# An RWKV-7 recurrence with a SoLU block: all chunk products in 64x64 tiles, transposes as products with the identity, banks taken in pairs

## The chip, the cores and the metric

One Trainium2 chip, and of it one core. The metric is the device time of one execution in microseconds (us). A core has a matrix engine (PE, which loads a stationary operand and streams a moving one, and writes to the PSUM banks), a vector engine (DVE), a scalar engine (ACT), a third elementwise engine (POOL), and queues that start DMA transfers (SP and ACT here). Each engine runs its instructions in the order in which they stand in its queue; semaphores tie the queues together.

## The reference

Inputs `r, k, v, w, a, b` have the shape (4 batches, 8 heads, 768 steps, 40). The first part is a recurrence over the steps, the second a block over 3072 tokens of width 320:

```python
for t in range(S):                       # state: (B, H, D, D)
    y[:, :, t] = einsum('bhd,bhde->bhe', rt, state)
    Sa = einsum('bhde,bhe->bhd', state, at)
    state = state * wt[:, :, None, :] - einsum('bhd,bhe->bhde', Sa, bt) + einsum('bhd,bhe->bhde', vt, kt)
x = y.transpose(0, 2, 1, 3).reshape(B * S, H * D)
h = x @ w_in                             # (320, 1024)
sm = softmax(h); solu = h * sm
ln = (solu - mean(solu)) / sqrt(var(solu) + 1e-6) * g_ln
out = ln @ w_out                         # (1024, 320)
```

The weights come as float64, and the kernel turns them into float32 itself.

## The kernel before, in words

Steps are cut into chunks of 64 (`C`). A **unit of work** is a pair of batches and one chunk: 128 partitions (two batches `p`, 64 steps each) by 8 heads. There are 2 x 12 = 24 such units (`N`), numbered i; i and i + 2 belong to the same pair of batches, so the state of i - 2 feeds i. Within a unit, 16 small products per step go over (p, head); a head is 4g + 2q + h in the kernel before.

The recurrence inside a chunk is solved in closed form. Per unit these helpers write the products, and PE runs them exactly in the order of the program (`manual_schedule`); the queues of DVE, ACT, POOL and SP are ordered by a scheduler when the program is built.

- `load_keys`, `load_values`: DMAs of w, b, k, a and of v, r, all from SP. `in_value_order`: three POOL copies that put v and r into the kernel's order of heads.
- `decay`: log of w (ACT), its running sum by a product with a triangle (bank `pcum`), its exponential (`inv`), the transposed running sum (`pex`) and its exponential (`ex`); POOL scales b and k (`kb`, line 285) and `front` sends that to DRAM (`kb_dram`).
- `front`: transposes b and a (`pbT`, `paT`, helper `turned`, line 291); ACT evicts `bT`, DVE evicts `aT` with a product (line 307).
- `norm`: products of b and a, masked by DVE (`nt`), written to DRAM and read back as `blk` in another layout (`spread`).
- `invert`: for every four units (`GRP`) DVE inverts 128 triangular 32x32 blocks by 30 rounds of `prod` (line 360) and `uu` (line 362); `bring` reads the results back as `tu` and `uh`, and `couple` (bank `py`) and `close` (bank `pz`) join the halves.
- `fetch`, `attend`: `kb` comes back as `kbx`; k, v, r are transposed (`pkT`, `pvT`, `prT`) and evicted by ACT. `scores`: their products (`ps`), masked by DVE into `psi` and the left part of `lv`. `states`: transposes the state (`psT`, line 518), evicted as `s`.
- `carried`, `driven` (bank `px`), `solved` (`pu`), `answered` (`pl`), `read` (`pyo`), `leave`: the solve, the output and the new state. `fence` is a drain of PE.
- `hidden` (`h`), `weighed`, `spreadof`, `folded` (`plnT`), `output` (`po`): the SoLU block of a unit that is done. It uses the whole 128x128 array, as the transposes do; the small products use the array as four 64x64 tiles.

A loop turn, called a **slot** here, does the stages of several units at once: `carried` to `leave` for unit i, `attend`, `couple`, `scores`, `close` for i + 1, `norm` for j = i + 7, `front` for j + 1, `decay` for j + 2, `hidden` for i - 1, `folded` and `output` for i - 2. PE's order in a slot before: px, pnt, px, plnT, pkT, pvT, prT, po, pu, py, h, pl, ps, pbT, paT, pcum, pex, psT, pyo, pz, pyo. A slot in which DVE has an inversion to do is called an inversion slot; inversions are started in slots 0, 4, 8, 12 and 16 (and one in the fill), and most of each runs in the slot after.

PSUM holds 8 banks of 512 floats per partition: `h` takes two, the other six go round among all the names above (`bank`, pool `ps1`). A product into a bank waits until the bank's last user has been read.

Of the kernel before, what the change touches and what calls it, by code (L numbers as in the profile page):

```python
# [45 lines left out]
def kernel(  # L46
# [34 lines left out]
    ps1 = ctx.enter_context(tc.tile_pool(name="ps1", bufs=6, space=PSUM))  # L81
# [32 lines left out]
    r_t = zeroed(nc.gpsimd, "r", [P, H, C], 2, pad)  # L114
    v_t = zeroed(nc.gpsimd, "v", [P, H, C], 2, pad)
# [12 lines left out]
    def bank(name):  # L128
        return ps1.tile([P, 512], FP32, tag="bank", name=name)
# [43 lines left out]
    def weights():  # L173
# [5 lines left out]
        pg = bank("pg")  # L179
# [6 lines left out]
        t = bank("pmean")  # L186
# [13 lines left out]
    units = [(p, g, q, h) for g in range(2) for p in range(2) for q in range(2) for h in range(2)]  # L200
# [16 lines left out]
    def pair(t, j):  # L217
        return t[:, j:j + 2, :].rearrange("p a b -> p (a b)")[:, 0:W2]
# [10 lines left out]
    def load(x, ap, i):  # L229
        bp, ci = where_(i)  # L230
        for p in range(2):
            nc.sync.dma_start(out=x[half(p), :, 0:D],
                              in_=ap[2 * bp + p, :, ci * C:(ci + 1) * C, :].rearrange("h t d -> t h d"))
# [5 lines left out]
    def load_keys(i):  # L239
        if not ok(i):  # L240
            return
        d = st[i]
        for n, ap in (("w", w), ("b", b), ("k", k), ("a", a)):
            x = a_t[i % 3] if n == "a" else two.tile([P, H, D], FP32, tag="raw_" + n, name="raw_" + n)
            d["raw_" + n] = x
            load(x, ap, i)

    def load_values(i):
        if not ok(i):
            return  # L250
        d = st[i]
        for n, ap in (("v", v), ("r", r)):
            d["raw_" + n] = two.tile([P, H, D], FP32, tag="raw_" + n, name="raw_" + n)
            load(d["raw_" + n], ap, i)

    def in_value_order(i):
        if not ok(i):
            return
        d = st[i]
        d["v"], d["r"] = v_t[i % 2], r_t[i % 2]  # L260
        d["lv"] = two.tile([P, H, W2], FP32, tag="lv", name="lv")
        for x, n in ((d["v"][:, :, 0:D], "raw_v"), (d["r"][:, :, 0:D], "raw_r"), (d["lv"][:, :, C:], "raw_v")):
            nc.gpsimd.tensor_copy(out=x.rearrange("p (h x) d -> p h x d", h=2),  # L263
                                  in_=d[n].rearrange("p (x h) d -> p h x d", h=2))


    def decay(i):
# [5 lines left out]
        t = bank("pcum")  # L273
        nc.tensor.matmul(heads(t[:, 0:DM]), lhsT=c_("cum"), rhs=lw[:, :, 0:D], start=True, stop=True)  # L274
        inv = two.tile([P, DM], FP32, tag="inv", name="inv", bufs=1)
        nc.scalar.activation(out=inv, in_=t[:, 0:DM], func=AF.Exp, scale=-1.0)  # L276
        t = bank("pex")
        for j in range(4):
            nc.tensor.matmul(t[0:W2, j * P:(j + 1) * P], lhsT=pair(lw, 2 * j), rhs=c_("cum"), start=True, stop=True)  # L279
        ex = d["ex"] = ex_t[i % (AHEAD + 3)]  # L280
        nc.scalar.activation(out=ex[0:W2, :, :, 1:].rearrange("p b j t -> p j b t"),
                             in_=t[0:W2].rearrange("p (j b t) -> p j b t", j=4, b=2), func=AF.Exp)
# [5 lines left out]
    def turned(name, src_, bufs=1, evict=True):  # L288
        t = bank("p" + name)
        for j in range(4):  # L290
            nc.tensor.transpose(out=t[0:W2, j * P:(j + 1) * P], in_=pair(src_, 2 * j), identity=ident)  # L291
        if not evict:
            return t
        o = two.tile([P, 4, P], FP32, tag=name, name=name, bufs=bufs)
        nc.scalar.copy(out=o[0:W2].rearrange("p j t -> p (j t)"), in_=t[0:W2])
        return o

    def front(i):
        if not ok(i):
            return  # L300
        d = st[i]
        nc.sync.dma_start(out=d["kb_dram"], in_=d["kbw"])
        ex = d["ex"]
        d["bT"] = turned("bT", d["kbw"][:, H:, :])
        t = turned("aT", d["raw_a"], evict=False)
        aT = d["aT"] = two.tile([P, 4, P], FP32, tag="aT", name="aT", bufs=AHEAD + 2)
        nc.vector.tensor_tensor(out=aT[0:W2].rearrange("p j (b t) -> p j b t", b=2),
                                in0=t[0:W2].rearrange("p (j b t) -> p j b t", j=4, b=2),
                                in1=ex[0:W2, :, :, 0:C].rearrange("p b j t -> p j b t"), op=ALU.mult)

    def masked(dst, t):
        nc.vector.tensor_tensor(out=dst, in0=t, in1=tri.unsqueeze(1).to_broadcast([P, 4, C]), op=ALU.mult)  # L312

    def keyed(t, i, u):
        p, g, q, h = u
        return t[rows(h), 2 * g + q, p * C:p * C + C]

    def valued(t, i, u):
        p, g, q, h = u
        return t[rows(q), 2 * h + g, p * C:p * C + C]  # L320

    def norm(i):
# [3 lines left out]
        t = [bank("pnt") for _ in range(2)]  # L326
        for u in in_turn(lambda p, g, q, h: (h, p ^ h)):
            p, g, q, h = u
            j = 2 * g + q
            mm(t[h][half(p ^ h), j * C:j * C + C], keyed(d["bT"], i, u), keyed(d["aT"], i, u))  # L330
        nt = d["nt"] = two.tile([P, 2, 4, C], FP32, tag="nt", name="nt", bufs=AHEAD + 1)
        for h in range(2):
            masked(nt[:, h], t[h][:, 0:256].rearrange("p (j c) -> p j c", j=4))
        d["nt_dram"] = dram.tile([P, H, C], FP32, tag="nt_dram", name="nt_dram", bufs=3)
# [35 lines left out]
    def bring(i):  # L370
# [6 lines left out]
        for x in range(2):  # L377
# [4 lines left out]
            nc.sync.dma_start(out=d["uh"][hi],  # L382
                              in_=uu[at + 16 + 8 * x:at + 24 + 8 * x, :, Q:].rearrange("h s t -> s h t"))

    def fetch(i):
# [3 lines left out]
        d["kb"] = two.tile([P, 2 * H, C], FP32, tag="kbx", name="kbx")  # L389
        nc.sync.dma_start(out=d["kb"], in_=d["kb_dram"])  # L390

    def couple(i):
# [3 lines left out]
        t = [bank("py") for _ in range(2)]  # L396
        for u in in_turn(lambda p, g, q, h: p ^ h):
            p, g, q, h = u
            j, x = 2 * g + q, half(p ^ h)
            mm(t[h][x, j * Q:j * Q + Q], d["nt"][x, h, j], d["tu"][x, 4 * h + j, 0:Q])  # L400
        for h in range(2):
            nc.scalar.activation(out=wy[:, h, :, 0:Q], in_=t[h][:, 0:4 * Q].rearrange("p (j c) -> p j c", j=4),
                                 func=AF.Copy, scale=c_("neg_hi"))

    def close(i):
# [3 lines left out]
        t = [bank("pz") for _ in range(2)]  # L409
        for u in in_turn(lambda p, g, q, h: p ^ h):  # L410
            p, g, q, h = u
            j, x = 2 * g + q, half(p ^ h)
            mm(t[h][x, j * Q:j * Q + Q], wy[x, h, j], d["uh"][x, 4 * h + j])
        for h in range(2):
            nc.scalar.copy(out=d["tu"][:, 4 * h:4 * h + 4, 2 * Q:], in_=t[h][:, 0:4 * Q].rearrange("p (j c) -> p j c", j=4))


    def attend(i):
# [3 lines left out]
        d["kT"] = turned("kT", d["kb"][:, 0:H, :])  # L422
        d["vT"] = turned("vT", d["v"])
        d["rT"] = turned("rT", d["r"], bufs=2)

    def scores(i):
# [3 lines left out]
        t = [bank("ps") for _ in range(2)]  # L430
        for u in in_turn(lambda p, g, q, h: (h, p)):
            p, g, q, h = u
            j = 2 * g + q
            mm(t[h][half(p), j * C:j * C + C], keyed(d["kT"], i, u), keyed(d["aT"], i, u))
        for u in in_turn(lambda p, g, q, h: (q, p)):
            p, g, q, h = u
            j = 4 + 2 * h + g
            mm(t[q][half(p), j * C:j * C + C], valued(d["vT"], i, u), valued(d["rT"], i, u))
        psi = d["psi"] = two.tile([P, 2, 4, C], FP32, tag="psi", name="psi")
        for x in range(2):  # L440
            masked(psi[:, x], t[x][:, 0:256].rearrange("p (j c) -> p j c", j=4))
        for x in range(2):
            masked(d["lv"][:, x::2, 0:C], t[x][:, 256:].rearrange("p (j c) -> p j c", j=4))


    def carried(i):
# [5 lines left out]
        d["px"] = [bank("px") for _ in range(2)]  # L452
        d["opened"] = set()
        if ci:
            for u in in_turn(lambda p, g, q, h: (h, p ^ h)):
                p, g, q, h = u
                j = 2 * g + q
                mm(d["px"][h][half(p ^ h), j * D:j * D + D], keyed(d["aT"], i, u),
                   st_t[bp][rows(h), 4 * p + j, 0:D], start=(h, p ^ h) not in d["opened"], stop=False)
                d["opened"].add((h, p ^ h))  # L460
            fence()

    def driven(i):
# [3 lines left out]
        for u in in_turn(lambda p, g, q, h: (p, p ^ h)):  # L467
            p, g, q, h = u
            j = 2 * g + q
            mm(d["px"][h][half(p ^ h), j * D:j * D + D], d["psi"][half(p), h, j],  # L470
               d["lv"][half(p), 4 * h + 2 * g + q, C:], start=(h, p ^ h) not in d["opened"])
            d["opened"].add((h, p ^ h))
        for h in range(2):
# [261 lines left out]
```

## Time and profile before

| | us |
|---|---|
| median of the runs | 824.64 (811.89 to 824.88, three runs) |
| the profiled execution | 821.3 |
| its span, first to last instruction | 819.5 |
| PE busy | 644.9 (79% of the span) |
| DVE, ACT, POOL busy | 379.0, 239.8, 168.4 |
| mean granted PE clock | 0.863 of full |

Every slot has one group of `pl` products, so their starts mark the slots. In the profile `pl` of unit 0 starts at 159.49, of unit 1 at 186.97, of unit 16 at 598.50, of unit 23 at 784.40. That cuts the span in four: a fill with one whole slot (187.0), 15 slots with everything in them (411.5, 27.4 each), 7 slots in which `norm`, `front` and `decay` have run out (185.9, 26.6 each), and a tail of 35.1.

A line of the timeline reads: start, length, engine, line, operation, output<-inputs, shape, how many were merged into the line, and in brackets how long the engine stood idle before and what released it. Matmuls overlap, so the step from one line's start to the next is what a group costs PE, not its length. A float32 product is two PE instructions; a PE transpose is one.

### The profile page before, as it was taken

The page shows a single profiled execution, that of the slowest core. Times are in us where ns is not written, and L with a number is a line of the kernel's source. Part 1 is how long each engine was busy: PE and PEld are TensorE (multiplying, and loading weights), DVE is VectorE, ACT ScalarE, POOL GpSimd, SP SyncE. Part 2 cuts the span into 40 slices and gives each one's busy share as a digit, 9 for nine tenths or more (in the row PEclk, how much of TensorE's full clock was granted, in tenths as well). Part 3 has the DMA queues.
Part 4 walks back from the last instruction along what each step waited for, and adds up shares of the span by engine and source line. Part 5 has one row for each costly group of instructions (what it writes and reads, how often), then busy time and mean ns, then how long its engine had stood idle before and what let it go on. Part 6 is the DMA issues. An engine that isn't in the chain of part 4 may idle for free.

```text
span 819.5 us, 26810 instructions
## 1 busy us (share of the span) xinstructions
PE 644.9 (79%) x11545; PEld 480.8 (59%) x11545; DVE 379.0 (46%) x1048; ACT 239.8 (29%) x592; POOL 168.4 (21%) x237
## 2 busy tenths in 40 slices
PE   4505506778989989889889899798997877989894
PEld 3304404657757766667667667676765665666652
DVE  3563572478403692343954228822479133123322
ACT  3323102323324322433234334133321222223121
POOL 6664234313202211221022102301111110000000
PEclk8655756669989989999989999799997789899997
DMA  7546847364464545554625655265422412011000
GB/s 149 145 133 138 204 109 191 64 138 95 96 169 108 111 79 129 155 122 89 146 80 115 152 133 127 49 161 125 97 70 52 120 47 54 23 52 41 15 20 13
DMA packets 224901, 84.31 MB, mean 103 GB/s; under 512 B 206088, under 2 KB 213136, under 8 KB 224016
## 3 DMA queue, kind: packets, MB, share of 16 engines
q1 hardware_dynamic: 220272, 76.12, 40.4%
q10 hardware_dynamic: 4512, 6.48, 2.7%
q8 instruction: 91, 1.49, 0.7%
q14 instruction: 26, 0.21, 0.1%
HBM read 49.53 MB, written 29.10 MB: 96 GB/s over the span
## 4 chain that ended last, share of the span: by engine, by line
PE 46%; DVE 23%; DMA 15%; issue 5%; POOL 5%; ACT 3%; SPq 2%; ACTq 0%; DVEq 0%; POOLq 0%
PE h L592 14%; PE po L642 10%; DMA kbx<-kb_dram 7%; DVE prod L360 5%; DVE uu L362 5%; PE pz L211 3%; PE pyo L211 3%; DVE e L604 3%; DVE nmax L595 3%; PE py L211 3%; DVE bs L612 2%; DMA uu_dram<-uu 2%; PE pu L211 2%; POOL n_s L143 2%; ACT e L598 2%
## 5 line engine op out<-in xcount | busy, mean ns | idle before, releaser
L595 DVE TENSOR_REDUCE nmax<-h 128x1 f32<-128x1024 f32 x24 | 29.4, 1223 | 305.0 <-PE h L592 305.0
L592 PE MATMUL h<-w_in,xT 120*128 120x512 f32 (+1 forms) x288 | 135.8, 622 | 0.0
L642 PE MATMUL po<-w,lnT 128*128 128x320 f32 x384 | 115.4, 456 | 3.9 <-ACT lnT L633 3.9
L642 PEld LDWEIGHTS po<-w,lnT 128*128 128x128 f32 x384 | 75.7, 203 | 34.9 <-ACT lnT L633 5.4
L592 PEld LDWEIGHTS h<-w_in,xT 120*128 120x128 f32 (+1 forms) x288 | 55.0, 197 | 62.2 <-issue 61.1
L598 ACT ACTIVATE e<-h,nmax 128x1024 f32<-128x1024 f32 x24 | 26.8, 1116 | 147.5 <-DVE nmax L595 147.5
L360 DVE TENSOR_TENSOR prod<-blk,uu 128x30 f32<-128x30 f32 (+9 forms) x180 | 62.9, 350 | 6.0
L362 DVE TENSOR_TENSOR uu<-uu,prod 128x30 f32<-128x30 f32 (+9 forms) x180 | 61.5, 342 | 5.7
L291 PE MATMUL pkT<-cst,kbx 128*104 128x128 f32 x96 | 18.7, 330 | 45.5 <-DMA kbx<-kb_dram 42.7
L621 POOL TENSOR_TENSOR rs<-c,mhalf 128x1 f32<-128x1 f32 x24 | 13.4, 557 | 188.7 <-DVE c L620 135.6
L285 POOL TENSOR_TENSOR kb<-raw_b,inv 128x320 f32<-128x320 f32 x24 | 20.9, 869 | 151.4 <-ACT inv L276 131.1
L291 PE MATMUL pbT<-cst,kb 128*104 128x128 f32 x96 | 18.4, 323 | 39.5 <-POOL kb L285 39.5
L263 POOL COPY v<-raw_v 128x320 f32<-128x320 f32 x24 | 10.9, 456 | 179.8 <-DMA raw_v<-in_v_dram 179.7
L274 PE MATMUL pcum<-lw,cst 128*128 128x320 f32 x48 | 24.6, 605 | 24.6 <-ACT lw L272 14.7
L211 PE MATMUL pyo<-lv,kbx 64*64 64x104 f32 x768 | 42.2, 268 | 0.5 <-DVE lv L312 0.4
L211 PE MATMUL pyo<-lu,kbx 64*64 64x104 f32 x768 | 41.0, 261 | 0.8 <-DVE lu L312 0.5
L291 PEld LDWEIGHTS pkT<-cst,kbx 128*104 128x104 f32 x96 | 12.2, 154 | 50.0 <-issue 46.9
L644 ACT ACTIVATE osb<-po,rs 128x320 f32<-128x320 f32 x24 | 12.7, 527 | 94.5 <-PE po L642 94.5
L211 PE MATMUL py<-tu,nt 64*64 64x32 f32 x768 | 30.6, 227 | 8.2 <-DMA tu<-uu_dram 6.0
L279 PEld LDWEIGHTS pex<-cst,lw 128*104 128x104 f32 x192 | 32.8, 223 | 7.0 <-issue 4.1
L474 ACT COPY x<-px 128x160 f32<-128x160 f32 x48 | 11.7, 295 | 83.7 <-PE plnT L632 25.4
L291 PEld LDWEIGHTS pbT<-cst,kb 128*104 128x104 f32 x96 | 11.4, 149 | 41.8 <-POOL kb L285 40.5
(105 smaller groups left out, 1253.1 us busy)
## 6 DMA issues: line engine op xcount, KB each, us to landing
kb_dram<-kb SPq DMA_DIRECT2D x24, 512.0 KB
kbx<-kb_dram SPq DMA_DIRECT2D x24, 512.0 KB
nt_dram<-nt SPq DMA_DIRECT2D x24, 256.0 KB
uu_dram<-uu SPq DMA_DIRECT2D x6, 1024.0 KB
raw_w<-in_w_dram SPq DMA_DIRECT2D x48, 80.0 KB
raw_b<-in_b_dram SPq DMA_DIRECT2D x48, 80.0 KB
raw_k<-in_k_dram SPq DMA_DIRECT2D x48, 80.0 KB
a<-in_a_dram SPq DMA_DIRECT2D x48, 80.0 KB
```

Of the source, the lines that this page charges most:

```text
L211: nc.tensor.matmul(o, lhsT=lhsT, rhs=rhs, start=start, stop=stop, skip_group_check=True)
L274: nc.tensor.matmul(heads(t[:, 0:DM]), lhsT=c_("cum"), rhs=lw[:, :, 0:D], start=True, stop=True)
L279: nc.tensor.matmul(t[0:W2, j * P:(j + 1) * P], lhsT=pair(lw, 2 * j), rhs=c_("cum"), start=True, stop=True)
L285: nc.gpsimd.tensor_tensor(out=kb[:, j * H:j * H + H, 0:D], in0=d["raw_" + n], in1=heads(inv), op=ALU.mult)
L291: nc.tensor.transpose(out=t[0:W2, j * P:(j + 1) * P], in_=pair(src_, 2 * j), identity=ident)
L360: nc.vector.tensor_tensor(out=t, in0=nb[:, j:j + 1, j + 1:Q].to_broadcast([P, j, m]), in1=u[:, 0:j, j:j + 1].to_broadcast([P, j, m]), op=A ...
L362: nc.vector.tensor_tensor(out=u[:, 0:j, j + 1:Q], in0=u[:, 0:j, j + 1:Q], in1=t, op=ALU.subtract)
L592: nc.tensor.matmul(h[:, hh], lhsT=d["xT"][0:n, kt, :], rhs=w_in[0:n, kt, hh], start=kt == 0, stop=kt == NK - 1)
L595: nc.vector.tensor_reduce(out=nmax, in_=h, axis=AX.X, op=ALU.max, negate=True)
L598: nc.scalar.activation(out=e, in_=h, func=AF.Exp, bias=nmax, accum_out=d["esum"])
L604: nc.vector.tensor_tensor(out=d["e"], in0=d["h"], in1=d["e"], op=ALU.mult)
L642: nc.tensor.matmul(o[:, 0:DM], lhsT=d["lnT"][:, f, :], rhs=w2[:, f, :], start=f == 0, stop=f == NF - 1)
```

## The change

- **Tiles.** The whole-array steps of the chunk work become 16 products of 64x64: each transpose is a product of the 64x64 block with a 64x64 identity (`turn`, `turned`), `pcum` becomes two products and `pex` 16. The state's transpose moves from `states` into `attend`. Only `plnT`, `h` and `po` still use the whole array, one after the other.
- **Banks.** `banks` hands out pairs of banks, three pairs in place of six single ones. Two tensors share a pair: k and v (`pkv`), r and the state (`prs`), a and b (`pa`), both halves of `plnT`. One instruction evicts both banks where there were two (masks, `nuT`, `lu`, `wy`, `tu`, `x`, `tot`).
- **Tiles of py and pz** alternate over four 64x64 tiles, not two.
- **Heads** are numbered 4q + 2g + h, so that v and r are loaded in place: `in_value_order` and its POOL copies go.
- **Buffers and transfers.** `kbx` gets a third buffer; `nt` is read back from DRAM (`ntx`) and not kept; `uh` is brought by four DMAs, not two; k and a of the first four units are loaded from ACT's queue.
- **Weights.** They are drawn at the start of slots 0 and 1, not in the fill.
- **Order on PE in a slot:** px, pnt, px, k, v (`pkv`), r, state (`prs`), a, b (`pa`), pcum, pex, pu, py, plnT, h, po, pl, ps, pyo, pz, pyo.

In the built program the second tensor of a shared pair waits for the eviction of the first: v's products for ACT's copy of `kT`, the state's for `rT`, b's for DVE's `aT`, the second half of `plnT` for the first `lnT`. DVE's queue in a normal slot is x, x, tot, nt, aT, nmax, e, the statistics, lu, psi, lv. In an inversion slot `aT` stands behind 12 of the 30 rounds, and `nmax` behind all of them.

```diff
-    ps1 = ctx.enter_context(tc.tile_pool(name="ps1", bufs=6, space=PSUM))
+    ps1 = ctx.enter_context(tc.tile_pool(name="ps1", bufs=3, space=PSUM))
-        return ps1.tile([P, 512], FP32, tag="bank", name=name)
+        return ps1.tile([P, 2, 512], FP32, tag="banks", name=name)
...
-        nc.tensor.matmul(heads(t[:, 0:DM]), lhsT=c_("cum"), rhs=lw[:, :, 0:D], start=True, stop=True)
+        for p in range(2):
+            mm(heads(t)[half(p)], c_("cum")[half(p), half(p)], lw[half(p), :, 0:D])
...
-    def turned(name, src_, bufs=1, evict=True):
-        t = bank("p" + name)
-        for j in range(4):
-            nc.tensor.transpose(out=t[0:W2, j * P:(j + 1) * P], in_=pair(src_, 2 * j), identity=ident)
...
+    def turn(t, to, of, at, x):
+        mm(t[half(to), of, at:at + C], x, ident[half(of), half(of)])
+    def turned(t, at, src_, keys):
+        for u in in_turn(lambda p, q, g, h: (p, h if keys else q)):
+            p, q, g, h = u
+            j = at + (2 * q + g if keys else 2 * g + h)
+            turn(t, h if keys else q, p, j * C, src_[half(p), head(u)])
+        return t[0:W2, :, at * C:at * C + 4 * C].rearrange("p b (j t) -> p b j t", j=4)
...
+        t = banks("pa")
+        a_ = turned(t, 0, d["raw_a"], True)
+        aT = d["aT"] = tokens("aT", AHEAD + 2)
+        nc.vector.tensor_tensor(out=aT[0:W2], in0=a_, in1=d["ex"][0:W2, :, :, 0:C], op=ALU.mult)
+        d["bT"] = kept("bT", turned(t, 4, d["kbw"][:, H:], True))
...
-        for u in in_turn(lambda p, g, q, h: p ^ h):
+        for u in in_turn(lambda p, q, g, h: (p ^ h, p)):
...
-        d["kT"] = turned("kT", d["kb"][:, 0:H, :])
-        d["vT"] = turned("vT", d["v"])
-        d["rT"] = turned("rT", d["r"], bufs=2)
+        t = banks("pkv")
+        d["kT"] = kept("kT", turned(t, 0, d["kb"], True))
+        d["vT"] = kept("vT", turned(t, 4, d["lv"][:, :, C:], False))
+        t = banks("prs")
+        d["rT"] = kept("rT", turned(t, 0, d["r"], False), 2)
...
-        d["kb"] = two.tile([P, 2 * H, C], FP32, tag="kbx", name="kbx")
+        d["kb"] = two.tile([P, 2 * H, C], FP32, tag="kbx", name="kbx", bufs=3)
...
+        t = banks("plnT")
         for x in range(2):
-            t = bank("plnT")
...
```

## The prediction, made before the changed kernel had run

> **What bounds the kernel now.** First the page: engine totals and clock.
>
> ```profile
> PE 644.9 (79%) x11545; PEld 480.8 (59%) x11545; DVE 379.0 (46%) x1048; ACT 239.8 (29%) x592; POOL 168.4 (21%) x237
> ...
> PEclk8655756669989989999989999799997789899997
> ```
>
> PE leads, but only after a sparse, half-clocked fill (first eight slices); later single slices lose clock. So next PE's timeline of one undisturbed slot (pu at 482.56 to pu at 507.71, 25.1 us), here its middle:
>
> ```profile
> 483.52 1.11 PE L211 MATMUL py<-tu,nt 64*64 64x32 f32 x32
> 484.56 5.42 PE L592 MATMUL h<-w_in,xT 120*128 120x512 f32 x12
> 489.92 0.69 PE L211 MATMUL pl<-rT,nuT 40*64 40x64 f32 x32
> 490.43 0.65 PE L211 MATMUL ps<-aT,kT 40*64 40x64 f32 x32
> 490.90 0.65 PE L211 MATMUL ps<-rT,vT 40*64 40x64 f32 x32
> 491.48 0.64 PE L291 MATMUL pbT<-cst,kb 128*104 128x128 f32 x4
> 491.96 0.60 PE L291 MATMUL paT<-cst,a 128*104 128x128 f32 x4
> ...
> 492.93 1.04 PE L279 MATMUL pex<-cst,lw 128*104 128x128 f32 x8
> 493.81 0.60 PE L518 MATMUL psT<-cst,st 128*104 128x128 f32 x4
> 494.79 0.69 PE L211 MATMUL pyo<-rT,s 40*64 40x64 f32 x32 [0.38 <-DVE lv L312]
> ```
>
> Read steps, not lengths: 32 instructions on four tiles cost 0.47 to 0.52, a transpose of a whole tensor 0.43 to 0.48, py on two tiles 1.04, pex 0.88, h 5.36. From psT to pyo 0.98 pass, of which 0.43 is psT: the eviction of `s` is waited for. PE sets the pace here.
>
> Third, an inversion slot, in stretches of the clock:
>
> ```profile
> 515.00:520.00 5.00, 2.70 (x105) 2.33 (x104) 4.66 (x12) 0.00 (x0) 0.92 (x2) 1.00 0.55 83
> 520.00:525.00 5.00, 3.41 (x42) 2.81 (x46) 4.95 (x11) 3.20 (x6) 1.68 (x2) 0.75 0.01 3
> 525.00:530.00 5.00, 4.78 (x113) 4.48 (x107) 4.27 (x18) 0.45 (x2) 0.94 (x2) 0.50 0.01 3
> 530.00:535.00 5.00, 4.88 (x114) 4.66 (x108) 2.10 (x8) 0.94 (x3) 2.67 (x3) 0.50 0.62 184
> ```
>
> Columns: stretch, length, busy time of PE, its weight loads, DVE, ACT, POOL, then clock. DVE (third) is full, PE waits 3.41 at 521.11 (pcum needs a bank whose mask is behind the inversion), and the clock is then halved for 14 us. Fourth, the waits:
>
> ```profile
> PE pkT L291 <- DMA kbx<-kb_dram: 42.7, 17, 13.5
> PE pbT L291 <- POOL kb L285: 39.5, 6, 26.5
> ```
>
> The first is spread over slots; the second's 26.5 is one wait in the fill, while POOL converts weights.
>
> **A full slot, part by part** (against 25.1).
> - Six transposes (0.43 to 0.48, sum 2.67) become six groups of 32 instructions at 0.52: +0.45. This takes the step of pu (0.52, same shape); at the py step they would cost 1.04 each.
> - pex 0.88 to 0.52: -0.36. pcum has no row on two tiles: two pairs side by side give the present 0.54, in series 1.07; I take 0.54, since px on the same four tiles runs in parallel.
> - py 1.04 to 0.52, pz 0.87 to 0.52: -0.87.
> - State turned early: psT's wait goes, -0.55. POOL writes the state well before (its update took 0.74 from 499.85, 1.7 into that slot).
> - `kbx` triple-buffered: its transfer starts a slot earlier; after plnT's 0.90, 1.07 passes before pkT (500.01 to 501.98). -1.07.
> - Six changes between whole array and tiles become two. ps to pbT shows 0.11 over ps's own step, po to pu 0.03: four fewer are worth 0.1 to 0.4; 0.25 taken.
> - Merged evictions save ACT and DVE about 0.15 a pair (two of 256 columns 0.74, one of 512 0.68); `in_value_order` saves POOL 1.4. Neither is late in a full slot, so nothing.
> - New waits, from the built program: the second tensor of a pair waits for the first's eviction. From the last issue to ACT's start takes 0.28 (pkT ends issuing at 502.41, kT starts 502.69), the copy 0.59 (kT), the way back at most 0.1: 0.95. v waits 0.95 for kT, the state 0.95 for rT, b 1.0 for aT (DVE 0.68); plnT's second half 1.25, because lnT stands behind nuT, lu and wy on ACT. Together 4.15. Behind each wait stands all of PE; nothing covers it. Bounds: 0 if the hardware finds the evictions done, 5 if ACT queues up.
>
> Sum: 25.1 + 0.45 - 0.36 - 0.87 - 0.55 - 1.07 - 0.25 + 4.15 = 26.6; walking the new queue item by item gives 26.5, which I use. After h, po (4.4), pl, ps and pyo's first part take 6.65; lu is ready 6.35 after h (nmax 1.22, e 1.11 on ACT, e 1.22, statistics 1.9, lu 0.68), so the later place of lu on DVE is just covered; 1 us more on DVE would be paid.
>
> The Trainium skill's page "TensorEngine Tiling (Array Packing)", under Performance Considerations, warns that tiling speeds up products but not the evacuation of PSUM. That speaks against this change; the row beside it is the 0.59 copy against 0.52 of products.
>
> **An inversion slot.** In the built program `aT` stands behind 12 rounds of inversion. Those took 8.0 (uu 58 at 501.88 to the end of prod 234 at 509.89); with x, tot and nt before them aT comes 10.7 into the slot. PE is ready for b at 6.2 and goes on at 11.4: 4.2 more than in a normal slot. Such a wait halves the clock (before: waits of 2.94, 3.56, 3.41, 3.95, 5.23, 5.85 and a pair of 1.2 were followed by 6.6, 7.7, 14, 20, 6.7, 10 and 8 us at half; a single 1.83 was not). Mean 10.4, so 5.2 lost. +9.4. `nmax`, behind all 30 rounds (22.9 of DVE), comes at 24.5, when h, delayed to 26, is not yet done.
>
> The Trainium skill's page "TensorE: Matmul & The Clock Gate", Part 1, has the clock back after about 3.4 us of sustained work. By that figure a stall would cost an estimated 1.7 and not 5.2, and the sum below would fall by about 14. The trace's stretches are longer, and I go by them.
>
> **The stages** (starts of `pl`).
> - Fill and slots 0, 1 (187.0). Without weights, units come every 9 (pcum at 69.2, 78.1, 88.0, 96.2: SP's issues, 0.65 a load, which remain), so the first inversion starts near 60 instead of 93, and py follows 34 later (92.96 to 126.76 before): 95. DVE then converts weights, queued behind the first psi: 12 of w_in at 2.7, 8 of w_out at 3.4, 60 in all. Slot 1's products wait for the last (pmean): it starts near 160 (before 166), is an inversion slot at low clock, and reaches pl 27 later: 187. Change 0, from -26 (the POOL wait vanishes and nothing comes back) to +15.
> - 15 full slots (411.5): 15 x 26.5 + 3 inversion slots x 9.4 + 4 left over from slot 1 = 430. +18.
> - 7 short slots (185.9): without pnt, a, b, pcum, pex and their waits 22.9, and 0.8 for `tu`, which SP brings after one more pair of issues: 23.7 each. In slot 17 nmax is 7 late, +10 with the clock. 176. -10. The waits for `kbx` there (5.23, 5.85) go.
> - Tail (35.1): plnT's wait once more, +1.
>
> Span 819.5 + 0 + 18 - 10 + 1 = 828.5; the profiled execution took 821.3 with its span, so 830. The median before (824.6) lies 3.3 above the profiled one, within the scatter of three runs.
>
> **Rivals.**
> - *Slower: the clock falls in every full slot.* From px to h, 10.6 long, PE works about 6 between waits of 0.95 to 1.25. Before, two waits of 1.21 and 1.23 with two py products between (232.7 to 235.4) halved the clock, and h took 8.2 instead of 5.4. At that price, 3.3 a slot with py, 15 slots add 50: 880; half of them, 855. It decides if two waits of about 1 a bare 0.5 apart count as one; 338 to 340, with 1.7 idle of 2, kept 1.00, which speaks against.
> - *Faster: the fill gives back 26.* If weights convert beside the first units and not after them, slot 1 starts near 135 and the time is 804. For it: POOL's 26.5 wait is only the weights' fault. Against: DVE's queue puts them behind the inversion.
> - *The products do not share the array*: at py's step, +0.52 for seven groups a slot, 15 slots: +55, 885. pu and ps, with the same shapes on four tiles, speak against.
>
> **Numbers.** Forecast 50% (815 to 845), clock 18%, fill 30% (790 to 812), no sharing 2%. About 2% (808 to 841) can be told from no change. Of the forecast 5 in 50 lie below, 10 above; of the fill case 20 in 30 below. So faster 25%, same 45%, slower 30%. Range 796 to 865, which leaves out the dearer half of the clock case and the cheapest fifth of the fill; the forecast's own is 815 to 845.
>
> **What would show it.** In the profile after: `pkv` with kT as releaser, near 0.95, 24 times; `pa` waiting 5 in five slots, followed by half clock; plnT's second half waiting for lnT; pkT's DMA wait gone; py at half its step; slots of 26.5. A clock below 1 in normal slots is the first rival; pl of unit 1 near 160 the second. Wrong at the root would be slots below 25, that is, shared pairs that cost nothing.

## The result, and the profile after

The changed kernel took 905.09 us (median of 4 runs, 899.92 to 907.86) against 820.18 before (four runs, one more than above): a ratio of 1.111, 95% interval 1.102 to 1.121. Times are medians of all runs of a kernel; the ratios leave out runs more than 1.5% above its fastest (two of `spread`, whose profile is of one of them, and one each of `weights_early` and `one_wait`). The forecast was 830, with 796 to 865 as the range; the rival "the clock falls in every full slot" stood at 855 to 880. The time lies beyond all of them, on the slower side, to which the prediction gave 30%.

First the page of the changed kernel: engine totals, clock, the instruction queue, and the chain.

```profile
PE 661.7 (73%) x16145; PEld 497.5 (55%) x16145; DVE 369.9 (41%) x882; ACT 236.8 (26%) x472; POOL 142.0 (16%) x189
...
PEclk8755557566899798798789779779687977998989
...
q8 instruction: 127, 2.08, 1.0%
...
PE 51%; DVE 12%; DMA 10%; issue 9%; ACT 7%; POOL 5%; SPq 4%; ACTq 1%; POOLq 0%; DVEq 0%
```

DVE, ACT and POOL have less to do than before, and PE's busy time hardly rose, yet its share fell from 79% to 73%. The clock line, mostly 9s after the fill before, is now a mix of 7s, 8s and 9s. ACT and "issue" (PE waits for nothing that the profile shows) now have 7% and 9% of the chain, from 3% and 5%. PE has 16145 matmul instructions in place of 11545. Next, what PE waited for (total us, times, longest):

```profile
PE pkv L211 <- ACT kT L298: 34.0, 24, 10.1
...
PE pa L211 <- DVE aT L309: 25.2, 19, 5.3
PE plnT L625 <- ACT lnT L626: 20.1, 24, 1.3
...
PE prs L211 <- ACT rT L298: 18.0, 22, 1.1
...
PE pkv L211 <- issue: 8.5, 7, 2.9
PE px L211 <- issue: 8.1, 10, 1.6
```

The first four are the waits inside the shared bank pairs, 97 us together. The long rows of before (42.7 for `kbx`, 39.5 for `kb`) have shrunk to 31.0 and 8.9. New are pauses marked "issue", 33.8 us in all against 4.7 before. One full slot (394.66 to 425.73), the lines of PE's timeline that begin after an idle time:

```profile
400.30 0.46 PE L211 MATMUL pnt<-aT,bT 40*64 40x64 f32 x14 [0.52 <-issue]
...
403.04 1.13 PE L211 MATMUL pkv<-cst,lv 64*64 64x64 f32 x32 [1.01 <-ACT kT L298]
...
405.27 0.70 PE L211 MATMUL prs<-cst,r 64*64 64x64 f32 x16 [0.67 <-issue]
406.76 1.13 PE L211 MATMUL prs<-cst,st 64*64 64x64 f32 x32 [0.79 <-ACT rT L298]
...
409.56 1.14 PE L211 MATMUL pa<-cst,kb 64*64 64x64 f32 x32 [0.81 <-DVE aT L309]
...
415.67 0.66 PE L625 MATMUL plnT<-cst,e 128*128 128x128 f32 x4 [0.91 <-ACT lnT L626]
```

Six gaps of 0.5 to 1.0 us, none of them long. The windows of that stretch, cut at 3.41 us for a reason that follows (PE busy is the second number, PEclk the third from the end):

```profile
395.84:399.26 3.42, 3.28 (x194) 3.18 (x187) 2.10 (x5) 0.37 (x1) 0.55 (x1) 1.00 0.12 32
399.26:402.67 3.41, 2.14 (x108) 1.72 (x100) 1.64 (x4) 0.69 (x2) 0.88 (x2) 1.00 0.22 68
402.67:406.08 3.41, 2.26 (x64) 1.97 (x64) 0.00 (x0) 0.96 (x3) 0.00 (x0) 0.50 0.18 36
406.08:409.50 3.42, 1.99 (x64) 1.83 (x64) 0.69 (x1) 1.12 (x2) 0.00 (x0) 0.50 0.52 129
409.50:412.91 3.41, 3.35 (x92) 2.83 (x96) 0.00 (x1) 1.55 (x4) 0.52 (x1) 0.50 0.54 93
```

A window with 1.27 idle is followed by half clock; it lasts for three windows, 10.2 us, until one of them is full. PE was busy for 7.6 of these, and half of that, 3.8, is lost, on top of 4.7 of gaps. So the short gaps cost nearly twice their length.

Where the 82.5 us between the two spans came from, by the stages of the prediction: fill with slots 0 and 1 +12.9 (`pl` of unit 1 at 199.91, before 186.97), 15 full slots +69.0, 7 short slots +4.5, tail -4.0. For the 14 slots from `pl` of unit 1 to `pl` of unit 15, I cut each trace into half-microsecond windows and split PE's time: work (busy times clock), clock loss (busy times what is missing from full clock), idle, and in the idle the pauses marked "issue". All in us:

| kernel | length | work | clock loss | idle | of it pauses |
|---|---|---|---|---|---|
| before | 387.7 | 331.9 | 16.8 | 39.0 | 1.5 |
| after | 453.2 | 311.4 | 60.4 | 81.4 | 21.8 |

The matrix work did fall, by 1.46 a slot. Clock loss rose by 3.1 a slot, idle by 3.0.

### The profile page after: what moved, and what is told of

The parts are those of the page before. It is cut to its first block, busy times and chain, and to the rows that moved or that the text cites. A ratio compares the mean times of both kernels' runs of the same rounds, so it can differ in the third digit from the quotient of the medians.

```text
span 902.0 us, 35700 instructions
## 1 busy us (share of the span) xinstructions
PE 661.7 (73%) x16145; PEld 497.5 (55%) x16145; DVE 369.9 (41%) x882; ACT 236.8 (26%) x472; POOL 142.0 (16%) x189
## 4 chain that ended last, share of the span: by engine, by line
PE 51%; DVE 12%; DMA 10%; issue 9%; ACT 7%; POOL 5%; SPq 4%; ACTq 1%; POOLq 0%; DVEq 0%
PE h L585 14%; PE po L635 10%; PE pyo L211 5%; PE pu L211 3%; PE prs L211 3%; DVE prod L361 3%; DVE uu L363 3%; PE pkv L211 2%; PE plnT L625 2%; PE pa L211 2%; POOL n_s L143 2%; PE ps L211 2%; DMA raw_k<-in_k_dram 2%; ACT lnT L626 1%; PE px L211 1%
## 5 line engine op out<-in xcount | busy, mean ns | idle before, releaser
L211 PE MATMUL pa<-cst,kb 64*64 64x64 f32 x768 | 25.7, 302 | 39.5 <-DVE aT L309 25.2
L309 DVE TENSOR_TENSOR aT<-pa,ex 104x512 f32<-104x512 f32 x24 | 16.5, 689 | 90.3 <-PE pa L211 79.8
L211 PE MATMUL pkv<-cst,kbx 64*64 64x64 f32 x768 | 22.5, 255 | 39.9 <-DMA kbx<-kb_dram 31.0
L625 PE MATMUL plnT<-cst,e 128*128 128x128 f32 x192 | 35.5, 314 | 20.6 <-ACT lnT L626 20.1
L211 PE MATMUL pkv<-cst,lv 64*64 64x64 f32 x768 | 25.2, 294 | 34.3 <-ACT kT L298 34.0
L211 PEld LDWEIGHTS pa<-cst,kb 64*64 64x64 f32 x768 | 21.5, 204 | 43.8 <-POOL kb L279 19.9
L211 PEld LDWEIGHTS pkv<-cst,lv 64*64 64x64 f32 x768 | 20.7, 196 | 38.4 <-ACT kT L298 37.9
L211 PEld LDWEIGHTS pkv<-cst,kbx 64*64 64x64 f32 x768 | 18.5, 162 | 41.2 <-issue 22.4
L597 DVE TENSOR_TENSOR e<-h,e 128x1024 f32<-128x1024 f32 x24 | 29.4, 1225 | 28.7 <-ACT e L591 28.7
L211 PE MATMUL pcum<-lw,cst 64*64 64x320 f32 x96 | 29.0, 692 | 14.4 <-ACT lw L263 14.4
```

Of the source, the lines that this page charges most:

```text
L211: nc.tensor.matmul(o, lhsT=lhsT, rhs=rhs, start=start, stop=stop, skip_group_check=True)
L309: nc.vector.tensor_tensor(out=aT[0:W2], in0=a_, in1=d["ex"][0:W2, :, :, 0:C], op=ALU.mult)
L597: nc.vector.tensor_tensor(out=d["e"], in0=d["h"], in1=d["e"], op=ALU.mult)
L625: nc.tensor.transpose(out=t[:, x, j * P:(j + 1) * P], in_=d["e"][:, f * P:(f + 1) * P], identity=ident)
```

## The experiments

Theory A: the four waits on shared pairs, and the clock that they trip. Theory B: PE runs out of instructions in the long stretch of small products, and these pauses trip it. A third question was the fill.

**Pairs turned before they are evicted** (`both_turned`). The same for r and the state, a and b, and the two halves of `plnT`:

```diff
-        d["kT"] = kept("kT", turned(t, 0, d["kb"], True))
-        d["vT"] = kept("vT", turned(t, 4, d["lv"][:, :, C:], False))
+        k_ = turned(t, 0, d["kb"], True)
+        v_ = turned(t, 4, d["lv"][:, :, C:], False)
+        d["kT"] = kept("kT", k_)
+        d["vT"] = kept("vT", v_)
```

> Both tensors of a bank pair (k and v, r and the state, a and b, the two halves of plnT) are turned before the first eviction is issued, so that no turn waits for an eviction of its own pair. In the changed kernel these waits took 50.0 us in the 14 slots from pl(1) to pl(15) (3.6 a slot), pauses without a releaser 21.8 (1.6 a slot), and half clock cost 60.4 (4.3 a slot, against 1.2 before). Theory A: the waits trip the clock. They go, clock loss falls to 17 in these slots, a slot falls from 32.4 to about 25.7, and the whole to 790 to 805. Theory B: the pauses without a releaser trip the clock. The waits go but the clock loss stays near 60: slots of 28.8, the whole about 840 to 850.

Measured 849.51, ratio to before 1.037 (1.028 to 1.046): 56 us less than the changed kernel, and no further down than theory B had said. Yet the clock loss fell from 60.4 to 27.6, most of the way that theory A had said. What took the gain is in PE's timeline:

```profile
356.24 0.63 PE L211 MATMUL pkv<-cst,kbx 64*64 64x64 f32 x28 [2.12 <-issue]
...
359.58 0.63 PE L211 MATMUL pa<-cst,a 64*64 64x64 f32 x28 [1.25 <-issue]
...
363.30 0.27 PE L211 MATMUL pu<-tu,x 64*64 64x64 f32 x2 [0.72 <-issue]
```

The four waits are gone, and the pauses have grown from 33.8 to 75.8 us over the whole span. (Part of the wait for `aT` has moved: in four inversion slots `py` now waits for ACT's `bT`, 12.9 in all.) Count the matmul instructions between two of the pauses: 128 from the first to the second, 127 recorded from the second to the third. Of the 63 stretches between two pauses of 0.3 or more, 61 hold a multiple of 128, or up to 16 fewer (either a few records are missing, or other instructions count as well). With its weight load a matmul is two instructions, so the pauses stand where blocks of 256 end. The instruction queue's row says the same: 127 packets for 2 x 16145 = 32290 instructions, 254 each; before, 91 packets for 23090, again 254. Such a block of small products lasts 1.9 us at full clock; from pause to pause it was 3.3 and 3.7 here. The packets of that queue, 16 KB each, settle it: all 64 pauses of 0.3 or more in this trace end 1.2 to 1.6 us after one of them has landed, and only 4 of PE's 45 other waits of that length do.

**Full-array work split along the slot** (`spread`, with the waits left in; `both_spread`, with the pairs turned first as well). `hidden` is cut into its two halves of 512 columns:

```diff
+        folded(i - 2)
         attend(i + 1)
...
+        hidden(i - 1, 0)
         solved(i)
         couple(i + 1)
         some(3)
-        folded(i - 2)
-        hidden(i - 1)
+        hidden(i - 1, 1)
         weighed(i - 1)
-        output(i - 2)
...
         scores(i + 1)
+        output(i - 2)
```

> The changed kernel with its full-array work split up again along the slot: plnT before k, half of h before pu and half after py, po between ps and pyo; the evictions inside the pairs stay where they are. Longest stretch of small products about 230 and not 640. Theory A (the waits on shared pairs trip the clock): the four waits of 0.8 to 1.0 a slot stay, the clock still falls behind k, 885 to 905. Theory B (long stretches of small products run PE out of instructions, and those pauses trip the clock): the pauses (33.8 us over the whole) shrink to a few us, the clock loss falls by about 3 a slot, slots of 27.7, the whole 825 to 840.

Measured 879.45, ratio 1.064 (1.053 to 1.076) by its two faster runs, 865.90 and 873.82: between the two theories and nearer to A. In its profile the pauses shrank to 8.3 us, as theory B had it, but the four waits stayed, and a granted clock of 0.835 and 0.845 in these two runs, for 0.795 to 0.817 in the changed kernel and 0.847 to 0.859 with the pairs turned, says that some of the clock came back.

> Both edits: pairs turned before they are evicted, and full-array work split up along the slot. Theory A: the same as with the pairs alone, 790 to 805, within 1% of it. Theory B: 30 to 60 us below the pairs alone, since only here the pauses go as well, about 770 to 780.

Measured 822.54, ratio 1.006 (1.001 to 1.010): 27 below the pairs alone, more than theory A allowed and less than theory B. The pauses fell from 75.8 to 42.2, of which 10.4 have another cause (`pz`, below `best1`). Neither theory holds alone. Most of the added clock loss went with the waits, as A had it; but the waits also hid pauses, which more than doubled when the waits went: instructions come in while PE waits.

**Fewer PE instructions** (`fewer`): the pairs turned first, and a, b, k and `pex` done with fewer, larger instructions (k, not shown, by 8 transposes of 64 rows and two heads each).

```diff
-        for u in in_turn(lambda p, q, g, h: (p, h)):
-            p, q, g, h = u
-            j = 2 * q + g
-            mm(t[half(h), p, j * C:j * C + C], lw[half(p), head(u)], c_("cum")[half(p), half(p)])
+        for j in range(4):
+            mm(t[0:W2, 0, j * P:j * P + P], pair(lw, 2 * j), c_("cum"))
...
-        a_ = turned(t, 0, d["raw_a"], True)
-        b_ = turned(t, 4, d["kbw"][:, H:], True)
+        for x, src_ in enumerate((d["raw_a"], d["kbw"][:, H:])):
+            for j in range(4):
+                nc.tensor.transpose(out=t[0:W2, x, j * P:j * P + P], in_=pair(src_, 2 * j), identity=ident)
```

> The kernel with pairs turned before they are evicted, with fewer PE instructions for the same result: a and b are transposed on the whole array (4 instructions each for 32), k in rows of 64 (8 for 32), and pex is 8 for 32. A full slot has about 580 matmul instructions for 682, that is 4.5 for 5.3 blocks of 128; the matrix work itself changes by less than 0.3 us a slot (pex 0.88 for 0.52, transposes 0.45 for 0.52). Theory S (PE gets its instructions in blocks of 256, a matmul and its weight load counting two, and a run of small products uses them up faster than they come): pauses without a releaser fall from 71 us to 30 to 40, and stand at multiples of 128 matmuls again; 800 to 820 (849.5 with the pairs alone). Rival: the pauses hang on a semaphore or on a place of the program and not on the number of instructions: about 70 us of them stay, 843 to 855.

Measured 819.35, ratio 1.001 (0.997 to 1.005): 30 below the pairs alone, at the upper end of theory S. The pauses fell from 75.8 to 45.8 (forecast 30 to 40); all 35 stretches between those of 0.3 or more again hold a multiple of 128 or just fewer. Fewer instructions for nearly the same matrix work (316.5 for 313.5 in the 14 slots) gave the time, so it is the number that counts. Not all of the saving arrives: in the 14 slots 27.6 of pauses went but the length fell by only 8.6, as other idle time rose by 12 and clock loss by 4. The fill gained 7.4 and the short slots 11.3.

**Weights drawn before slot 0** (`weights_early`), everything else as changed:

```diff
-        if i == 0:
-            drawn(20)
-        if i == 1:
-            drawn(100)
...
+        if -4 <= i < 0:
+            drawn(9)
         read(i, True)
...
+        if i == 0:
+            drawn(100)
         bring(i + 2)
```

> The changed kernel with the weights drawn where the kernel before drew them, in the four slots before slot 0 and at its end. Everything else as changed. If the late weights hold slot 1 (PE waits 18.6 us for them in pmean; slot 1 takes 56.1 us), pl(1) moves from 199.9 to 185 or less and the whole falls by 13 to 25, to 880 to 892. Rival: the fill is bound by loads and by the wait for kbx (31 us), pl(0) moves from 143.8 to about 160 and pl(1) stays within 5 us of 199.9: the whole within 1% of 905.

Measured 895.95, ratio 1.093 (1.083 to 1.103); the interval touches that of the changed kernel, and the time lies between the two forecasts. `pl` of unit 0 moved from 143.8 to 163.9 and of unit 1 only from 199.9 to 196.6, as the rival had it. The late weights cost 3.3 us in the fill and 9 by the median of the whole; the earlier slot 0 paid for most of the later slot 1.

**All of it** (`best1`): pairs turned first, full-array work split, fewer instructions, early weights.

> All of it together: pairs turned before they are evicted, full-array work split up along the slot, fewer PE instructions as in the run before this, and the weights drawn before slot 0. Theory S: the pauses left with pairs and split (42 us) fall to about 20, weights give 3 to 9: 785 to 805. Rival: what is left is not the number of instructions, and only the weights' part is gained: 813 to 822.

Measured 787.14, ratio 0.963 (0.957 to 0.970): faster than both kernels. Its page, the same rows as above:

```profile
PE 625.9 (80%) x13649; PEld 448.4 (57%) x13649; DVE 370.8 (47%) x882; ACT 227.4 (29%) x472; POOL 144.3 (18%) x189
...
PEclk9755555688799997999997999979999799999998
...
q8 instruction: 107, 1.75, 0.9%
...
PE 57%; DMA 13%; DVE 12%; issue 7%; POOL 4%; SPq 4%; ACT 1%; ACTq 0%; DVEq 0%; POOLq 0%
```

The 9s are back, ACT is off the chain (1%), and 107 packets again hold 255 instructions each. The 14 slots, worked out as above (`spread` is left out):

| kernel | length | work | clock loss | idle | of it pauses |
|---|---|---|---|---|---|
| both_turned | 415.7 | 313.5 | 27.6 | 74.5 | 54.3 |
| both_spread | 393.2 | 312.5 | 32.2 | 48.5 | 31.5 |
| fewer | 407.1 | 316.5 | 31.8 | 58.7 | 26.6 |
| best1 | 380.0 | 316.5 | 26.4 | 37.1 | 23.1 |

Not every pause marked "issue" is one for instructions. In `best1` four, 11.5 us in all and three of them in the 14 slots, stand before `pz` in inversion slots:

```profile
413.71 0.68 DVE L317 TENSOR_TENSOR lv<-ps,cst 128x512 f32<-128x512 f32 x1
...
414.50 1.08 PE L211 MATMUL pz<-uh,wy 64*64 64x32 f32 x32 [3.12 <-issue]
```

With `po` moved behind `ps`, `pz` is the third pair after `ps` and so gets the same banks. It has to wait until DVE, held up by the inversion, has read them: all four start 0.10 after the end of DVE's `lv`. Without them the pauses of `best1` are 19.7 us over the whole span, the "about 20" of theory S.

**One and two waits put back into the fastest version** (`one_wait`, `two_waits`). This asks what trips the clock. In the traces a grid of 3.4135 us fits all 51 changes of the changed kernel's clock within 0.02 us. Hence the windows above.

```diff
+        d["kT"] = kept("kT", k_)
         v_ = turned(t, 4, d["lv"][:, :, C:], False)
-        d["kT"] = kept("kT", k_)
```

> The fastest version so far (787.1) with one of the changed kernel's four waits put back: kT is evicted before v is turned, so v waits for it once a slot, 24 times about 0.8, together 19 us. In the traces so far the clock changes only on a grid of 3.41 us; it falls after a window in which PE was idle for about 40% or more, and comes back after one that was some 80 to 100% busy. Theory W (the idle time summed over a window decides): 0.8 in 3.41 is 24%, the clock keeps: 800 to 812, clock loss in the slots from pl(1) to pl(15) stays at 26 plus or minus 6. Theory L (every wait of 0.8 trips the clock): 3 us more a slot, 850 or above.

Measured 807.75, ratio 0.983 (0.973 to 0.994), within theory W's range and far from theory L. Clock loss in the 14 slots 34.2, just above what W allowed; waits of 30.6 us cost 21, while the pauses fell from 31.2 to 20.6.

```diff
-        r_ = turned(t, 0, d["r"], False)
+        d["rT"] = kept("rT", turned(t, 0, d["r"], False), 2)
...
-        d["rT"] = kept("rT", r_, 2)
```

> The same with two of the waits put back, v for kT and the state for rT, with about 1 us of products between them: 46 waits, 37 us. Theory W: both together are 1.6 in some 2.6 us; a window that holds both is about 47% idle, at the limit, so the clock falls in part of the slots, 1 to 2 us a slot on top of the waits: 835 to 870, clock loss from pl(1) to pl(15) 40 to 55. Rival (the longest single wait decides, and 0.8 is too short): the waits alone, 818 to 828, clock loss as with one wait.

```profile
PE pkv L211 <- ACT kT L299: 31.5, 24, 2.1
PE prs L211 <- ACT rT L299: 18.6, 22, 0.9
```

Measured 834.79, ratio 1.021 (1.014 to 1.029): a hair below W's range, above the rival's. The second wait cost 27 us for 18.6 of waiting; clock loss rose from 34.2 to 39.3 in the 14 slots, just under W's range. These 14 slots of single traces do not tell the first wait from the second (+7.8 and +5.1). The whole span of the same traces does, with a loss of 65.3, 68.4 and 80.9 us for no wait, one and two, and so does a count: of the 14 slots, 6 had no half clock in `best1`, 6 with one wait, 3 with two, 1 with all four (the changed kernel, whose work is also less spread).

**plnT moved into the longest stretch of small products** (`best2`):

```diff
         norm(j)
+        folded(i - 2)
         driven(i)
...
-        folded(i - 2)
         attend(i + 1)
```

> The fastest version so far with plnT moved from behind px to ahead of the second px group, in the middle of the run of small products between po and k (224 matmul instructions long there). Theory S (supply of instructions): the pauses at px, pnt and prs, 14 us in the whole, shrink by half, 780 to 786. Rival: 0.9 us of plnT is too short to bring in another block, within 0.5% of 787.

Measured 788.78, ratio 0.965 (0.960 to 0.970), the same as the fastest. The rival holds: 0.9 us of `plnT` buys nothing there.

## Why the prediction was wrong, point by point

- *Work of a full slot: right.* The terms for transposes, `pex`, `py`, `pz` and mode switches sum to -1.03; measured -1.46.
- *The waits that go: right in sum, one of them by luck.* Neither the wait behind psT nor pkT's for `kbx` appears in these slots of the changed kernel. The latter had been 9.8 us in 14 slots, 0.7 each, not 1.07. The former was misread: that psT turned the next unit's state, and pyo did not wait for its eviction, which in the slot shown ended at 495.14, after pyo had begun (494.79). It began 0.05 after the first of DVE's two `lv` masks, which its line names as the releaser, had read a bank of `ps`:

```profile
494.32 0.75 DVE L312 TENSOR_TENSOR lv<-ps,cst 128x256 f32<-128x256 f32 x2
494.56 0.58 ACT L522 COPY s<-psT 104x512 f32<-104x512 f32 x1
```

In the changed kernel pyo follows ps directly and gets the next pair, not that of ps, so that wait is gone wherever the state is turned.
- *The new waits: right.* Forecast 4.15 a slot by the rows of ACT and DVE. In the 14 slots they took 50.0, 3.57 a slot: `aT` 0.99, `lnT` 0.89, `kT` 0.86, `rT` 0.83.
- *The clock in a normal slot: the step that failed.* The forecast priced the slot with the clock at 1.00 throughout, and held against the rival that "338 to 340, with 1.7 idle of 2, kept 1.00". The loss was 4.3 a slot against 1.2 before, close to the rival's price of 3.3 a slot more. Its condition, two waits close enough to count as one, was not the right one, though: no gap needs to be long, their sum in one window of the grid counts. The stretch I relied on lies in a window with PE busy for 1.58 of 3.41, after which the clock stayed full, a rare exception (last section):

```profile
338.19:341.60 3.41, 1.58 (x14) 1.53 (x14) 0.00 (x0) 2.07 (x6) 0.00 (x0) 1.00 0.81 247
341.60:345.01 3.41, 3.41 (x14) 2.38 (x14) 0.00 (x0) 0.76 (x2) 0.00 (x0) 1.00 0.84 320
```

`both_turned` shows what the waits did: without them, the loss is 27.6 and not 60.4.
- *Pauses for instructions: missed altogether, put at nothing* by the forecast and all rivals. 11545 matmul instructions stood on the page of before, and the count after could be had from the built program, but I priced only their time on the array. In the 14 slots they cost 21.8, and in `both_turned`, with the waits gone, 54.3. So the sign to look for in "slots below 25" could not have come even with pairs that cost nothing. They are also of the size of what lies beyond the rival's 880.
- *Inversion slots: mis-sized.* +9.4 forecast for each, for `aT` behind 12 rounds. The three inversion slots between units 1 and 15 took 33.6 on average, the others 32.0: +1.6. b waited for `aT` 1.69, 2.28 and 0.91, not 5. PE came later to b than I had it, since its own waits had delayed it, and the clock was halved in normal slots too.
- *The fill: 0 forecast, +12.9.* Slot 1 took 56.1 and PE waited 18.6 there for weights, as the forecast's working had it in kind; but `pl` of unit 1 came at 199.9 and not 187. Drawing the weights early recovers 3.3 of it. Of the rest, 5.2 is slot 1's own length, 32.7 for 27.5 in that run, and 4.4 the later slot 0.
- *Short slots and tail: -10 and +1 forecast, +4.5 and -4.0.* In the short slots the matrix work fell by 5.3, but idle time rose by 6.0 and clock loss by 3.9: three of the four waits are there too, and the pauses.
- *Products that do not share the array: rightly at 2%.* The groups of 32 ran at 0.47 to 0.52 where the clock was full.

Shown by runs: the waits and the clock they trip cost 56 us net of the pauses they hid; instructions and their spread are worth a further 62 (849.5 to 787.1, the weights with them); several short waits together lose the clock. Not settled: why a block sometimes takes longer to come (pauses of 0.3 to 4.7). Whether the transfers of data slow those of instructions was not tried.

## What to carry to other kernels

A wait that is shorter than a microsecond has to be priced with the others around it: sum PE's idle time over a few microseconds, not gap by gap. When two tensors share a bank pair, write both before the first is evicted; and count instructions as well as their time, because cutting a transpose into sixteen small products leaves the array's time alone but asks for eight times the instructions. Where removing a wait gains less than its length, look for a second limit that the wait was covering.

## What the runs showed of the hardware

**The clock changes on a fixed grid.** In each of 11 traces all changes between full and half lie within 0.02 us of a grid of 3.4135 us. I took PE's busy share of every window from `pl` of unit 1 to `pl` of unit 23 and asked for the clock of the next:

| busy share of the window | full: next half / full | half: next half / full |
|---|---|---|
| below 0.4 | 58 / 0 | 13 / 0 |
| 0.4 to 0.5 | 55 / 3 | 4 / 0 |
| 0.5 to 0.6 | 34 / 52 | 21 / 0 |
| 0.6 to 0.7 | 12 / 84 | 34 / 0 |
| 0.7 to 0.8 | 2 / 130 | 85 / 0 |
| 0.8 to 0.9 | 0 / 108 | 17 / 11 |
| 0.9 and above | 0 / 1020 | 50 / 150 |

It mostly takes about half a window of idle time to lose the clock, and a window that is nearly full to have it back. So gaps of 20%, harmless at full clock, hold it at half. The Trainium skill's page "TensorE: Matmul & The Clock Gate", Part 1, has a free-running window of 4096 cycles, 3413 ns; the grid of these traces agrees with it. The shares are this case's.

**Instructions come in blocks of 256,** and a run of small products on four tiles outruns them: 1.9 us of use against 3.3 to 3.7 from pause to pause. In none of the 11 traces do two packets of PE's instruction queue land less than 3.27 us apart, though one packet takes only 0.9 to 2.1. Leaving out those of `pz`, 241 of the 248 pauses of 0.3 or more in these traces end 1.15 to 1.7 us after such a landing; of PE's 775 other waits of that length 59 do. The Trainium skill's page "Runtime: NRT & Kernel Launch", section "Instruction fetch mechanics", has the blocks of 256 too, but calls the cost of crossing one mostly hidden. Here it was not: 75.8 of 847 us in `both_turned`.
